# One tag for each buffer of a ring, and a last output chunk that is copied in halves and sent by two queues

## The chip, the core and the metric

The kernel runs on one core of one Trainium2 chip. The core has a matrix engine (TensorE, PE in the profile, with its weight loads as PEld), a vector engine (VectorE, DVE), a scalar engine (ScalarE, ACT), a general engine (GpSimd, POOL) and SyncE (SP), which here issues the DMAs. Each engine works through its own list of instructions in order and waits at semaphores for the others. The metric is the device time of one execution in microseconds; smaller is better.

## The reference

```python
def _attn_ref(q, k, v):                        # q, k, v: 8 batches x 8 heads x 1152 x 64
    q_pool = q.reshape(B, H, S // 2, 2, D).mean(axis=3)
    scores = (1.0 / np.sqrt(D)) * np.matmul(q_pool, k.transpose(0, 1, 3, 2))
    attn = np.exp(scores - scores.max(-1, keepdims=True))
    attn = attn / (attn.sum(-1, keepdims=True) + 1e-09)
    return np.matmul(attn, v)                  # 8 x 8 x 576 x 64

def _moe_ref(x, w_gate, wq, wk, wv, wo):       # x: 8 x 576 x 512, the heads side by side; 4 experts
    logits = x @ w_gate                        # the two best experts of a row, softmax over the two
    for e in range(E):
        q, k, v = x @ wq[e], x @ wk[e], x @ wv[e]          # 576 x 64 each
        a = softmax(causal(q @ k.T / np.sqrt(64)))
        out += weight[e] * (a @ v @ wo[e])     # weight is 0 where e is not among the two best
    return out                                 # 8 x 576 x 512, float32
```

## The kernel before, in words

The first stage is pooled attention. The 64 heads go in 32 pairs; a pair fills the 128 partitions with two heads of 64. For each pair the kernel finds row maxima (`f_max`, reduced by VectorE at line 572), computes transposed scores of nine key chunks (`f_st`, TensorE through `rows2`, line 325), takes exponentials on ScalarE into tiles named `pt` (line 666), multiplies them by v (`f_av`, TensorE through `cols2`, line 332) and adds up the `pt` tiles on GpSimd into `sacc` (line 349), from which the denominators come. `f_xfin` ends a half of a pair: ScalarE copies the accumulator out of PSUM into `accs`, TensorE sums `sacc` into a bank (called den here, line 332), VectorE transposes, inverts and multiplies it there (lines 722 to 734 and 345), ScalarE casts it into `x` and VectorE subtracts that cast from the same bank to get the low half of `x` (line 345). Only then is the bank of den free.

After every four pairs a batch of the second stage starts (`start_moe`): projections of x (`f_qk`, `f_vproj`, 12 matmuls at line 316 into one bank for each group), row maxima with the causal mask (`f_mmax`, line 956), scores, exponentials, products and at last the output projection (`f_out`). This work is laid between the attention work of the next four pairs.

All results of TensorE go to one ring of eight PSUM banks, `gen`, and all exponentials to one ring of eleven SBUF buffers, `pt`. A ring is an object of the kernel, and so is a planner: while the program is written out, `emit` keeps a clock for each engine and a time of last use for each buffer, and the main loop at the end of the kernel picks the next piece of work by these clocks and by the tables HEAD, CYCLE and TAIL. `Ring.new` takes the buffer that by the planner's clocks comes free first, `min(self.slots)`, and then asks the tile pool for a tile:

```python
r = Res(self.pool.tile(self.shape, self.dt, tag=self.tag, name=f"{self.tag}_{self.n}", bufs=self.bufs), self)
```

All buffers of a ring have one tag here, so which of the eight banks the tile really gets is the pool's choice and not the planner's. The first instruction that writes into the new tile waits until the last user of the old tile in that bank is done.

The output of the last batch is written by `f_out` in its tail form: a chunk of 128 rows is projected in two steps of three matmuls, ScalarE copies the 128x512 result into a `pt` buffer, and SyncE issues its DMA through `mv`. Chunks 2, 3 and 4 come last, in this order. Chunk 4 is made of 64 rows of the last batch and 64 of the one before, and so goes out in two DMAs of 64 rows.

Of the kernel before, what the change touches and what calls it, by code (L numbers as in the profile page):

```python
# [17 lines left out]
SQ = 576  # L18
# [6 lines left out]
DM = 512  # L25
# [9 lines left out]
AC0, ACL, ACT = 0.1, 0.8, 0.8  # L35
# [69 lines left out]
class Res:  # L105
# [15 lines left out]
        return self.u + SEM[self.ue]  # L121

    def free(self):
        self.ring.slots.append((self.ru, self.u, self.ue))
        self.ring.live -= 1


class Ring:
    def __init__(self, pool, tag, shape, dt, bufs):
        self.pool, self.tag, self.shape, self.dt, self.bufs = pool, tag, shape, dt, bufs  # L130
        self.slots, self.live, self.n = [(0.0, 0.0, "")] * bufs, 0, 0

    def avail(self, k=1):
        return sorted(self.slots)[k - 1][0] if len(self.slots) >= k else INF
# [1 line left out]
    def new(self):  # L136
        t = min(self.slots)
        self.slots.remove(t)
        self.live += 1
        self.n += 1  # L140
        r = Res(self.pool.tile(self.shape, self.dt, tag=self.tag, name=f"{self.tag}_{self.n}", bufs=self.bufs), self)
        _, r.u, r.ue = t
        return r


# [15 lines left out]
def pooled_attention_then_moe_kernel(ctx: ExitStack, tc: tile.TileContext, qT, kT, vP, wall, wop, out):  # L161
    nc = tc.nc
# [172 lines left out]
    def act_copy(o, i, n, R, W, psum=True):  # L335
        nc.scalar.copy(o, i)  # L336
        emit("ACT", n / 1200 + (0.05 if psum else 0.083), R, W)
# [23 lines left out]
    def fl(ap):  # L361
        return ap.bitcast(F32) if ap.dtype == F32R else ap

    def mv(dst, src, R, W):
        d = fl(dst)
        nc.sync.dma_start(d, fl(src))
        n = 4
        for k in d.shape:
            n *= k
        emit("SP", 0.63, R, W, n / 250e3)  # L370

    def sp():
        return clk["SP"] - (SP0 if prog["f"] == 0.0 else SPL if prog["f"] < NP - 0.9 else SPT)
# [678 lines left out]
    def f_yfin(b, ep, qb, acc, sacc):  # L1052
# [12 lines left out]
        if k < qn:  # L1065
# [5 lines left out]
            yl, o = YL[b // 2], 64 * (b % 2)  # L1071
# [3 lines left out]
        YR[b, ep, qb] = yr  # L1075
        if b == NB - 1:
            if (b, 1 - ep, qb) not in YR:
                for t in ((0, 1), (2, 3, 4))[qb]:
                    spawn("out", f_out(b, (t,), (ep, 1 - ep)), m_prio(b, 3))
        elif qb == 0 and (b, 1 - ep, 0) in YR:  # L1080
            spawn("out", f_out(b, range(4 + b % 2), (0, 1)), m_prio(b, 3, "C"))
# [4 lines left out]
    def f_out(b, ts, eps):  # L1086
        tail = b == NB - 1
        ro = r_pt if tail else r_ob
        for t in ts:
# [4 lines left out]
            ps, ob = r_gen.new(), ro.new()  # L1094
            o = ob.ap.rearrange("p a b -> p (a b)")[:, 0:DM] if tail else ob.ap
            for i, ep in enumerate(eps):
                if i and tail:
                    yield (lambda: yr(ep), "C")
                for k, (yi, W) in enumerate(((0, OH), (1, OH), (0, OL))):
                    l = YL[b // 2][:, ep, yi, :] if t == 4 else Y[b, ep][:, yi, 128 * t:128 * t + 128]  # L1100
                    mm(ps.ap, l, W[:, ep, :], i + k == 0, i == 1 and k == 2, 0.233, [YR[j, ep, q] for j in bs], [ps])
            m_prog[b] += 1.4
            act_copy(o, ps.ap, DM, [ps], [ob])
            ps.free()
            for i, j in enumerate(bs):
# [95 lines left out]
```

## Time and profile before

| | us |
|---|---|
| median of three runs | 1204.38 (1204.35 to 1204.39) |
| profiled execution, whole time | 1205.93 |
| profiled execution, span of the trace | 1204.2 |
| TensorE busy | 1158.4 (96%) |
| GpSimd busy | 972.0 (81%) |
| VectorE busy | 860.6 (71%) |
| ScalarE busy | 704.5 (58%) |
| mean granted TensorE clock | 0.996 of full speed |

The trace covers 1204.2 of the 1205.93 us of its execution; the median of the runs is 1.55 us below that execution. A row of the timeline gives start and duration in us, engine, line, operation, output<-inputs, shapes, how many instructions were merged, and in brackets the idle time of the engine ahead of it with the engine and line whose event ended it. A busy engine still need not be the one that sets the end, so the idle time of TensorE and the chain of work that ended last are read beside the shares.

### The profile page before, as it was taken

What the parts mean: (1) busy time and instruction counts of PE and PEld (TensorE: products, weight loads), DVE (VectorE), ACT (ScalarE), POOL (GpSimd) and SP (SyncE); (2) the same over time, 40 slices, a digit from 0 to 9 for tenths busy, and PEclk for the clock granted to TensorE, in tenths of its full rate; (3) what the DMA queues carried; (4) which work ended last, traced back from release to release, by engine and by line L of the source; (5) the groups of instructions that cost most, each with busy time, mean ns of one, the idle gap of its engine ahead of it and who ended that gap; (6) DMA issues with size and microseconds to landing.
All of it is one profiled execution on the core that took longest, in us unless ns stands there. A gap on an engine that the chain in (4) does not pass through costs nothing.

```text
span 1204.2 us, 29456 instructions
## 1 busy us (share of the span) xinstructions
PE 1158.4 (96%) x11233; PEld 892.0 (74%) x11233; DVE 860.6 (71%) x2113; ACT 704.5 (58%) x2036; POOL 972.0 (81%) x844
## 2 busy tenths in 40 slices
PE   6999999999999999999999999999999999999997
PEld 5676886778876787767886777866877677877785
DVE  7988667767676767777677776776767876577265
ACT  5676545765466654665556754566646665465624
POOL 4999978797699966999669987699786996889912
PEclk9999998999999999999999999999999999999999
DMA  4232212022211212122111221112211122200001
GB/s 158 80 102 69 61 54 67 16 66 76 61 54 55 69 48 61 54 60 92 32 41 54 85 82 30 44 47 85 78 41 34 60 65 87 61 15 9 8 29 45
DMA packets 40426, 70.30 MB, mean 58 GB/s; under 512 B 4871, under 2 KB 31453, under 8 KB 40285
## 3 DMA queue, kind: packets, MB, share of 16 engines
q1 hardware_dynamic: 40284, 68.43, 18.5%
q8 instruction: 88, 1.44, 0.5%
q14 instruction: 54, 0.43, 0.1%
HBM read 58.73 MB, written 9.44 MB: 57 GB/s over the span
## 4 chain that ended last, share of the span: by engine, by line
PE 61%; POOL 27%; DVE 5%; ACT 3%; issue 3%; DMA 1%; POOLq 0%; SPq 0%; DVEq 0%; ACTq 0%
PE gen L325 24%; POOL sacc L349 23%; PE gen L316 19%; PE gen L332 17%; POOL kl L349 3%; ACT pt L666 2%; POOL pt L1018 1%; DVE gen L956 1%; DVE PM L572 1%; DVE ql L345 1%; ACT pt L999 1%; PE gen L622 0%; DVE gen L734 0%; DMA qraw<-in_qT 0%; DVE gen L345 0%
## 5 line engine op out<-in xcount | busy, mean ns | idle before, releaser
L349 POOL TENSOR_TENSOR sacc<-sacc,pt 128x640 f32<-128x640 f32 (+4 forms) x588 | 828.2, 1413 | 128.6 <-ACT sacc L341 92.4
L572 DVE TENSOR_REDUCE PM<-gen 128x1 f32<-128x384 f32 x864 | 425.6, 549 | 168.7 <-PE gen L325 140.3
L666 ACT ACTIVATE pt<-gen 128x320 f32<-128x320 f32 (+1 forms) x1152 | 381.4, 432 | 137.1 <-PE gen L325 126.9
L332 PE MATMUL gen<-pt,v 128*64 128x320 f32 (+4 forms) x2752 | 355.7, 402 | 1.7 <-POOL pt L1018 0.5
L332 PEld LDWEIGHTS gen<-pt,v 128*64 128x64 f32 (+1 forms) x2752 | 192.1, 137 | 138.9 <-issue 11.8
L325 PE MATMUL gen<-qh,kh 64*128 64x320 f32 (+1 forms) x1152 | 211.8, 316 | 2.7 <-ACT accs L336 1.1
L325 PE MATMUL gen<-qh,kl 64*128 64x320 f32 (+1 forms) x1152 | 196.3, 297 | 0.0
L325 PE MATMUL gen<-RM,ON 64*128 64x320 f32 (+1 forms) x1152 | 191.6, 292 | 0.8 <-ACT RM L336 0.8
L325 PE MATMUL gen<-ql,kh 64*128 64x320 f32 (+1 forms) x1152 | 191.3, 293 | 0.0
L325 PE MATMUL gen<-kh,qh 64*128 64x384 f32 x768 | 157.1, 368 | 7.4 <-ACT qh L336 7.1
L325 PEld LDWEIGHTS gen<-qh,kh 64*128 64x128 f32 x1152 | 132.8, 185 | 33.8 <-issue 11.3
L325 PEld LDWEIGHTS gen<-RM,ON 64*128 64x128 f32 x1152 | 130.4, 186 | 1.2 <-ACT RM L336 1.0
L325 PEld LDWEIGHTS gen<-ql,kh 64*128 64x128 f32 x1152 | 129.8, 186 | 0.0
L325 PEld LDWEIGHTS gen<-qh,kl 64*128 64x128 f32 x1152 | 127.4, 186 | 0.0
L325 PEld LDWEIGHTS gen<-kh,qh 64*128 64x128 f32 x768 | 88.2, 187 | 38.1 <-issue 16.3
L316 PE MATMUL gen<-x,WH 128*128 128x320 f32 (+1 forms) x512 | 104.9, 299 | 7.4 <-DVE x L345 7.4
L349 POOL TENSOR_TENSOR kl<-kraw,kh 128x384 fp32r<-128x384 f32 x96 | 95.5, 1013 | 9.5 <-ACT mqh L336 3.4
L956 DVE CUSTOM_DVE_ANT_0 gen<-gen,mqk 64x288 f32<-64x288 f32 (+4 forms) x160 | 74.7, 503 | 25.6 <-PE gen L325 24.4
L316 PEld LDWEIGHTS gen<-x,WH 128*128 128x128 f32 x512 | 82.2, 188 | 10.6 <-issue 9.7
L332 PE MATMUL gen<-sacc,ones 128*64 128x320 f32 (+1 forms) x384 | 66.1, 425 | 13.8 <-POOL sacc L349 13.3
L336 ACT CAST x<-gen 128x256 fp32r<-128x256 f32 x64 | 25.8, 403 | 86.9 <-DVE gen L345 86.8
L316 PE MATMUL gen<-x,WL 128*128 128x320 f32 (+1 forms) x256 | 75.6, 295 | 0.0
(116 smaller groups left out, 1573.5 us busy)
## 6 DMA issues: line engine op xcount, KB each, us to landing
kraw<-in_kT SPq DMA_DIRECT2D x96, 192.0 KB
v<-in_vP SPq DMA_DIRECT2D x96, 192.0 KB
qraw<-in_qT SPq DMA_DIRECT2D x31, 576.0 KB
out<-ob SPq DMA_DIRECT2D x28, 256.0 KB
wst<-in_wall SPq DMA_DIRECT2D x8, 193.0 KB
out<-pt SPq DMA_DIRECT2D x4, 256.0 KB
RM<-nt SPq DMA_DIRECT2D x62, 2.5 KB
out<-ob SPq DMA_DIRECT2D x6, 128.0 KB
```

Source lines behind the costliest of these rows:

```text
L316: nc.tensor.matmul(o, lhsT, rhs, start=start, stop=stop)
L325: nc.tensor.matmul(o(j), l(HEAD[j]), r(HEAD[j]), start=i == 0, stop=i == len(terms) - 1)
L332: nc.tensor.matmul(o(HEAD[j]), l(j), r(j), start=start, stop=stop)
L336: nc.scalar.copy(o, i)
L345: nc.vector.tensor_tensor(o, a, b, op=op)
L349: nc.gpsimd.tensor_tensor(o, a, b, op=op)
L572: nc.vector.tensor_reduce(pm[:, i, t:t + 1], ps[:, :384], axis=AX.X, op=ALU.max)
L666: nc.scalar.activation(pts[i][:, j, :qn], st[j][:, qn * i:qn * i + qn], AF.Exp, scale=0.0625)
L956: nc.vector.tensor_tensor_reduce(p, p, mqk[:m, 384 + m - w:384 + m], 1.0, LOW, ALU.add, ALU.max, pm[:m, j, c, i:i + 1])
L999: nc.scalar.activation(pt_[:kn, j, f:qn], st[j][:kn, o - n:o], AF.Exp, scale=0.125)
L1018: nc.gpsimd.affine_select(out=sq, in_=sq, compare_op=ALU.is_ge, fill=0.0, base=0, pattern=[[0, 2], [1, kn]], channel_multiplier=-1)
```

## The change

Two things are changed.

The tag of a tile is now made of the ring's name and the number of the buffer that the ring chose, with one buffer for each tag. So the tile gets exactly the buffer that `min(self.slots)` names. To keep that number, a slot is a tuple of four, and `free` hands it back. The shapes and the number of buffers stay as they were. In the built programs 787 of the 2472 `gen` tiles and 97 of the 693 `pt` tiles follow another tile in their buffer than before; in all other rings each tile follows the same one. The work on each engine stands in the same order as before up to the last output chunks.

In the tail the chunks go in the order 2, 4, 3, so that a chunk of 128 full rows comes last. Its result is copied in halves of 256 columns, the first by ScalarE and the second by VectorE; SyncE sends the first half and ScalarE's own queue the second.

```diff
--- before.py
+++ after.py
@@ -121,14 +121,14 @@
         return self.u + SEM[self.ue]
 
     def free(self):
-        self.ring.slots.append((self.ru, self.u, self.ue))
+        self.ring.slots.append((self.ru, self.u, self.ue, self.slot))
         self.ring.live -= 1
 
 
 class Ring:
     def __init__(self, pool, tag, shape, dt, bufs):
         self.pool, self.tag, self.shape, self.dt, self.bufs = pool, tag, shape, dt, bufs
-        self.slots, self.live, self.n = [(0.0, 0.0, "")] * bufs, 0, 0
+        self.slots, self.live, self.n = [(0.0, 0.0, "", i) for i in range(bufs)], 0, 0
 
     def avail(self, k=1):
         return sorted(self.slots)[k - 1][0] if len(self.slots) >= k else INF
@@ -138,8 +138,9 @@
         self.slots.remove(t)
         self.live += 1
         self.n += 1
-        r = Res(self.pool.tile(self.shape, self.dt, tag=self.tag, name=f"{self.tag}_{self.n}", bufs=self.bufs), self)
-        _, r.u, r.ue = t
+
+        r = Res(self.pool.tile(self.shape, self.dt, tag=f"{self.tag}{t[3]}", name=f"{self.tag}_{self.n}", bufs=1), self)
+        _, r.u, r.ue, r.slot = t
         return r
 
 
@@ -361,13 +362,13 @@
     def fl(ap):
         return ap.bitcast(F32) if ap.dtype == F32R else ap
 
-    def mv(dst, src, R, W):
+    def mv(dst, src, R, W, by="SP"):
         d = fl(dst)
-        nc.sync.dma_start(d, fl(src))
+        (nc.sync if by == "SP" else nc.scalar).dma_start(d, fl(src))
         n = 4
         for k in d.shape:
             n *= k
-        emit("SP", 0.63, R, W, n / 250e3)
+        emit(by, 0.63, R, W, n / 250e3)
 
     def sp():
         return clk["SP"] - (SP0 if prog["f"] == 0.0 else SPL if prog["f"] < NP - 0.9 else SPT)
@@ -1075,7 +1076,7 @@
         YR[b, ep, qb] = yr
         if b == NB - 1:
             if (b, 1 - ep, qb) not in YR:
-                for t in ((0, 1), (2, 3, 4))[qb]:
+                for t in ((0, 1), (2, 4, 3))[qb]:
                     spawn("out", f_out(b, (t,), (ep, 1 - ep)), m_prio(b, 3))
         elif qb == 0 and (b, 1 - ep, 0) in YR:
             spawn("out", f_out(b, range(4 + b % 2), (0, 1)), m_prio(b, 3, "C"))
@@ -1100,6 +1101,17 @@
                     l = YL[b // 2][:, ep, yi, :] if t == 4 else Y[b, ep][:, yi, 128 * t:128 * t + 128]
                     mm(ps.ap, l, W[:, ep, :], i + k == 0, i == 1 and k == 2, 0.233, [YR[j, ep, q] for j in bs], [ps])
             m_prog[b] += 1.4
+            if tail and t == 3:
+
+                hs, w = [Res(None), Res(None)], DM // 2
+                act_copy(o[:, :w], ps[:, :w], w, [ps], [hs[0]])
+                nc.vector.tensor_copy(o[:, w:], ps[:, w:])
+                emit("DVE", w / 960 + 0.07, [ps], [hs[1]])
+                for i, by in enumerate(("SP", "ACT")):
+                    mv(out[b * SQ + 128 * t:b * SQ + 128 * t + 128, w * i:w * i + w], o[:, w * i:w * i + w], [hs[i]], [], by)
+                ps.free()
+                ob.free()
+                continue
             act_copy(o, ps.ap, DM, [ps], [ob])
             ps.free()
             for i, j in enumerate(bs):
```

Lines of the changed kernel are 1 to 12 higher than those of before from the second half of `Ring` on. In the rows below a name is a tile, the first number counts the tiles of its ring and the second is a running number; in brackets stand the semaphores that an instruction waits for.

The first place is on TensorE, about 313 us into the span, where a projection of batch 1 begins (`gen_659` and `gen_660` are its first two banks, after four maxima products of the batch before it). Before:

```order
L325 MATMUL gen_657_5019<-mkh_3_4475,mqh_3_4457 64x288 [waits DVE_49]
L325 MATMUL gen_658_5020<-mkh_3_4475,mqh_3_4457 64x288 [waits DVE_49]
L316 MATMUL gen_659_5029<-x_5_2154,WH_116 128x256 [waits DVE_49,PE_49]
L316 MATMUL gen_659_5029<-x_5_2154,WH_116 128x256
L316 MATMUL gen_659_5029<-x_5_2154,WL_117 128x256
L316 MATMUL gen_659_5029<-x_6_2863,WH_116 128x256 x2
L316 MATMUL gen_659_5029<-x_6_2863,WL_117 128x256
L316 MATMUL gen_659_5029<-x_7_3492,WH_116 128x256 x2
L316 MATMUL gen_659_5029<-x_7_3492,WL_117 128x256
L316 MATMUL gen_659_5029<-x_8_4095,WH_116 128x256 x2
L316 MATMUL gen_659_5029<-x_8_4095,WL_117 128x256
L316 MATMUL gen_660_5046<-x_5_2154,WH_116 128x320 [waits Activation_49]
```

and with the change:

```order
L326 MATMUL gen_657_5019<-mkh_3_4475,mqh_3_4457 64x288 [waits DVE_49]
L326 MATMUL gen_658_5020<-mkh_3_4475,mqh_3_4457 64x288 [waits DVE_49]
L317 MATMUL gen_659_5029<-x_5_2154,WH_116 128x256 [waits Activation_49]
L317 MATMUL gen_659_5029<-x_5_2154,WH_116 128x256
L317 MATMUL gen_659_5029<-x_5_2154,WL_117 128x256
L317 MATMUL gen_659_5029<-x_6_2863,WH_116 128x256 x2
L317 MATMUL gen_659_5029<-x_6_2863,WL_117 128x256
L317 MATMUL gen_659_5029<-x_7_3492,WH_116 128x256 x2
L317 MATMUL gen_659_5029<-x_7_3492,WL_117 128x256
L317 MATMUL gen_659_5029<-x_8_4095,WH_116 128x256 x2
L317 MATMUL gen_659_5029<-x_8_4095,WL_117 128x256
L317 MATMUL gen_660_5046<-x_5_2154,WH_116 128x320 [waits DVE_49]
```

The work is the same; the first matmul of `gen_659` waited for VectorE and TensorE and now waits for ScalarE, and that of `gen_660` waited for ScalarE and now waits for VectorE. In the built programs the bank of `gen_659` was that of `gen_652`, a den bank, and is now that of `gen_624`, an accumulator that ScalarE copies out; `gen_660` takes the den bank in its place. The same exchange stands at the first projection of batches 2 to 6 (`gen_968`, `gen_1276`, `gen_1585`, `gen_1893`, `gen_2202`).

The second place is on TensorE early in the kernel, at the scores of pair 4 about 109 us into the span (`gen_242` and `gen_243` take row maxima, `gen_244` and `gen_245` the scores of the two heads). Before:

```order
L325 MATMUL gen_242_1810<-kh_15_1480,qh_5_1374 128x384 [waits Activation_49]
L325 MATMUL gen_243_1811<-kh_15_1480,qh_5_1374 128x384 [waits Activation_49]
L325 MATMUL gen_244_1817<-qh_4_930,kh_10_710 128x320 [waits DVE_49]
L325 MATMUL gen_245_1818<-qh_4_930,kh_10_710 128x320 [waits DVE_49]
L325 MATMUL gen_244_1817<-qh_4_930,kl_10_1338 128x320
```

and with the change:

```order
L326 MATMUL gen_242_1810<-kh_15_1480,qh_5_1374 128x384 [waits Activation_49]
L326 MATMUL gen_243_1811<-kh_15_1480,qh_5_1374 128x384 [waits DVE_49]
L326 MATMUL gen_244_1817<-qh_4_930,kh_10_710 128x320 [waits Activation_49]
L326 MATMUL gen_245_1818<-qh_4_930,kh_10_710 128x320 [waits Activation_49]
L326 MATMUL gen_244_1817<-qh_4_930,kl_10_1338 128x320
```

The first matmuls of `gen_244` and `gen_245` waited for VectorE and now wait for ScalarE; with that of `gen_243` it is the other way round.

The third place is the end of the program. On SyncE, whose list holds the output DMAs (`pt_689` to `pt_693` are the five chunks of the last batch), the last five before:

```order
L366 DMA out_0<-pt_690_19203 128x512 [waits DMAHW0_49,Activation_49]
L366 DMA out_0<-pt_691_19225 128x512 [waits DMAHW1_49,Activation_49]
L366 DMA out_0<-pt_692_19230 128x512 [waits DMAHW2_49,Activation_49]
L366 DMA out_0<-pt_693_19235 64x512 [waits DMAHW3_49,Activation_49]
L366 DMA out_0<-pt_693_19235 64x512 [waits DMAHW4_49]
```

and with the change:

```order
L367 DMA out_0<-pt_690_19203 128x512 [waits DMAHW0_49,Activation_49]
L367 DMA out_0<-pt_691_19225 128x512 [waits DMAHW1_49,Activation_49]
L367 DMA out_0<-pt_692_19230 64x512 [waits DMAHW2_49,Activation_49]
L367 DMA out_0<-pt_692_19230 64x512 [waits DMAHW3_49]
L367 DMA out_0<-pt_693_19235 128x256 [waits DMAHW5_49,Activation_49]
```

The two DMAs of 64 rows now stand ahead of the last one, which carries half a chunk. ScalarE's list now ends with the DMA of the other half, behind its own copy of 128x256, and VectorE's list ends with a copy that it did not have:

```order
L735 STREAM_TRANSPOSE gen_2469_19207<-r9_96_19213 128x320 [waits DVE_49]
L346 TENSOR_TENSOR gen_2469_19207<-accs_96_19193,gen_2469_19207 128x320 [waits DVE_49]
L346 TENSOR_TENSOR y_16_19090<-gen_2469_19207,y_16_19090 128x256 [waits DVE_49,Activation_49]
L346 TENSOR_TENSOR yl_4_18031<-gen_2469_19207,yl_4_18031 128x64
L1108 COPY pt_693_19235<-gen_2472_19234 128x256 [waits Activation_49]
```

The last row is added; it waits for ScalarE.

## Rows read from the trace of the kernel before

**Rows 1.** The page: busy time, share of the span and instructions of each engine.

```profile
PE 1158.4 (96%) x11233; PEld 892.0 (74%) x11233; DVE 860.6 (71%) x2113; ACT 704.5 (58%) x2036; POOL 972.0 (81%) x844
```

**Rows 2.** The page: the chain that ended last, shares of the span by engine.

```profile
PE 61%; POOL 27%; DVE 5%; ACT 3%; issue 3%; DMA 1%; POOLq 0%; SPq 0%; DVEq 0%; ACTq 0%
```

**Rows 3.** Waits: engine, line and releaser; total us, times, longest us.

```profile
PE gen L332 <- POOL sacc L349: 13.3, 17, 1.6
PE gen L316 <- DVE x L345: 7.4, 6, 1.2
...
ACT pt L666 <- POOL sacc L349: 7.9, 9, 1.4
```

**Rows 4.** Timeline of all engines from 311.0 to 313.5 us.

```profile
311.10 1.82 DVE L345 TENSOR_TENSOR ql<-qraw,qh 128x576 fp32r<-128x576 f32 x1
...
311.40 0.76 PE L325 MATMUL gen<-mkh,mqh 64*128 64x512 f32 x6
311.55 0.43 ACT L336 COPY accs<-gen 128x320 f32<-128x320 f32 x1
312.84 0.41 DVE L345 TENSOR_TENSOR x<-gen,x 128x256 fp32r<-128x256 f32 x1
...
313.40 0.36 PE L316 MATMUL gen<-x,WH 128*128 128x256 f32 x1 [1.24 <-DVE x L345]
```

**Rows 5.** Timeline of TensorE at 314.8 us, where the second group begins.

```profile
314.89 0.31 PE L316 MATMUL gen<-x,WH 128*128 128x320 f32 x1
```

**Rows 6.** Timeline of GpSimd from 313 to 375 us, the rows with idle time.

```profile
324.60 0.23 POOL L871 TENSOR_TENSOR gate<-v,gate 128x20 f32<-128x20 f32 x1 [5.34 <-DVE gate L871]
...
330.40 1.27 POOL L349 TENSOR_TENSOR sacc<-sacc,pt 128x512 f32<-128x512 f32 x1 [1.24 <-ACT sacc L341]
```

**Rows 7.** Timeline of TensorE and its loads, single rows at five other places.

```profile
147.13 0.30 PEld L316 LDWEIGHTS gen<-x,WH 128*128 128x128 f32 x2 [0.28 <-DVE PM L572]
...
431.93 0.51 PE L316 MATMUL gen<-WH,x 128*128 128x260 f32 x2 [0.26 <-ACT pt L666]
...
723.26 0.30 PEld L316 LDWEIGHTS gen<-WH,x 128*128 128x128 f32 x2 [0.37 <-ACT pt L666]
...
1068.59 0.18 PEld L325 LDWEIGHTS gen<-mqh,mkh 64*128 64x128 f32 x1 [0.20 <-DVE PM L572]
...
1167.85 0.51 PE L316 MATMUL gen<-WH,x 128*128 128x260 f32 x2 [0.57 <-DVE MPM L956]
```

**Rows 8.** Timeline of TensorE from 108.6 to 112.2 us.

```profile
109.17 0.87 PE L325 MATMUL gen<-qh,kh 64*128 64x320 f32 x2
...
111.72 0.76 PE L332 MATMUL gen<-sacc,ones 128*64 128x320 f32 x4 [1.24 <-POOL sacc L349]
```

**Rows 9.** Timeline of ScalarE from 109 to 111 us.

```profile
110.08 0.77 ACT L666 ACTIVATE pt<-gen 128x320 f32<-128x320 f32 x2 [1.44 <-POOL sacc L349]
```

**Rows 10.** The chain in order of time, its last piece: start, us, what.

```profile
1199.63 0.58 ACT pt L336
```

**Rows 11.** Timeline from 1183 us on: copies of 128x256 out of PSUM.

```profile
1196.40 0.37 ACT L336 CAST y<-gen 128x256 fp32r<-128x256 f32 x1 [0.64 <-DVE gen L345]
...
1196.92 0.42 DVE L345 TENSOR_TENSOR y<-gen,y 128x256 fp32r<-128x256 f32 x1 [0.55 <-ACT yl L336]
```

**Rows 12.** Timeline of SyncE, the issues of the last three output DMAs.

```profile
1199.54 0.33 SPq L366 DMA_DIRECT2D out<-pt  x1
...
1200.24 0.55 SPq L366 DMA_DIRECT2D out<-pt  x1
...
1200.84 0.59 SPq L366 DMA_DIRECT2D out<-pt  x1
```

**Rows 13.** Line 366: issue durations in ns, least, median, most.

```profile
L366 SPq DMA_DIRECT2D out<-ob x34: 332/344/1426, 247.0 to 1149.7; - x34
```

**Rows 14.** Windows: busy time by engine, PEclk, DMA share, GB/s.

```profile
1200.50:1201.00 0.50, 0.00 (x0) 0.00 (x0) 0.00 (x0) 0.00 (x0) 0.00 (x0) 1.00 0.98 381
...
1202.50:1203.00 0.50, 0.00 (x0) 0.00 (x0) 0.00 (x0) 0.00 (x0) 0.00 (x0) 0.52 0.36 82
```

## The prediction

> **What bounds the kernel now.** I read the shares first: TensorE is busy 96% of the span, GpSimd 81%, VectorE 71%, ScalarE 58% [rows 1]. A busy share is an average, so the chain that ended last comes next: 61% of it is TensorE and 27% GpSimd [rows 2]. So there are stretches where TensorE sets the pace and others where it is GpSimd with its additions into `sacc`. A wait of TensorE that is taken away counts if nothing behind it runs into GpSimd. The third view is therefore who TensorE waits for [rows 3]. The longest group is 13.3 us in 17 waits for GpSimd's sums, which are data. The second is 7.4 us in 6 waits, 1.2 us each, in which the first matmul of a projection waits for VectorE's subtraction of the low half of x. That subtraction yields nothing that this projection reads: the low half belongs to a later pair. It is the last reader of a den bank, so this is a wait for a PSUM bank and not for data, and the choice of bank is what the change alters.
>
> **The change part by part.** *The six waits at the projections.* The timeline at the first of them shows the whole case [rows 4]. The last maxima matmul ends at 311.40 + 0.76 = 312.16. The projection starts at 313.40, after 1.24 us of idle time. VectorE is late because it first does an addition into `ql` of 1.82 us, and only then, from 312.84 to 313.25, the subtraction that frees the bank. The accumulator bank, which this tile gets now, is free when ScalarE's copy into `accs` is done, at 311.55 + 0.43 = 311.98, which is 0.18 us before TensorE gets there. So nothing of this wait is left: 6 x 1.24 = 7.4 us.
>
> What is late next? The den bank goes to the second group of the same projection. In the trace that group starts 314.89 - 313.40 = 1.49 us after the first [rows 4, 5]; without the wait it would start at 312.16 + 1.49 = 313.65. It can start 0.15 us after the bank is free (313.40 - 313.25 in the same rows), thus at 313.40. The cover is 0.25 us. If VectorE is later than that, the rest of its lateness comes back as a wait there. After that comes GpSimd: it is idle for 5.34 us up to 324.60 and again 1.24 us up to 330.40, waiting both times for work that hangs from these projections [rows 6], so it moves forward with TensorE. I take 7.4 whole.
>
> *The other `gen` tiles.* The built orders give 794 matmuls another wait than before, most of them in pairs that swap a bank freed by ScalarE for one freed by VectorE, a few tenths of a microsecond each, in both directions. Most of these gain or lose a little that the next wait for GpSimd's sums (17 of them [rows 3]) takes back, since its sums don't come earlier for it. I looked for places where the idle time before the matmul is ended by the user of the old bank, where the new one is long free, and where no such wait follows soon. There are five, with 0.28, 0.26, 0.37, 0.20 and 0.57 us of idle time, three of them on the loads and two on the matmuls [rows 7]. The sum is 1.68; a matmul behind an idle load loses somewhat less, so I take 1.4. The ends are 0 and 1.7.
>
> On the other side, at 109 us the new bank is worse. The scores of pair 4 start at 109.17 [rows 8]. Their new banks are freed by two exponentials, which ran from 110.08 to 110.85 because ScalarE had itself waited for GpSimd [rows 9]. That puts up to 1.7 us in TensorE's way. But 2.5 us later the same stretch ends in a wait of 1.24 us for GpSimd [rows 8], which doesn't get longer when TensorE comes later. And ScalarE's own wait there goes, see the next part. I take nothing for it; the ends are 0 and a loss of 1.7 - 1.24 = 0.5.
>
> *The `pt` tiles.* 97 of them change buffers. ScalarE waits 7.9 us in 9 waits for GpSimd to release a `pt` buffer [rows 3], and in the new program the waits of this kind name an addition that is older by up to four. ScalarE is busy 58% [rows 1], and TensorE has other work while an exponential is late, so I take nothing. The ends are 0 and a gain of 5.3, which is two thirds of those waits.
>
> *The tail.* Before: the last copy of 128x512 runs from 1199.63 to 1200.21 [rows 10]; SyncE issues chunk 3 at 1199.54, then the two halves of chunk 4 at 1200.24 (0.55 us) and 1200.84 (0.59 us) [rows 12]. Now chunk 4 stands where chunk 3 stood, so its two issues start at 1199.54 and end at 1199.54 + 0.55 + 0.05 + 0.59 = 1200.73. SyncE's half of chunk 3 follows at about 1200.77, against 1200.84 for the last issue before, so splitting the copy gains almost nothing on this queue: the queue is what is late. The issue itself covers 128 rows; such an issue takes 0.33 us, and one of 64 rows up to 0.59 [rows 12]: 0.26 less. For the other half, ScalarE's copy of 128x256 takes 0.37 us and ends at 1200.00. VectorE's copy waits for it, so the halves are not copied at the same time; with 0.42 [rows 11] it ends near 1200.45, and ScalarE issues at about 1200.5, done near 1200.8. That is ahead of SyncE's. So the gain is between 0.07 and 0.07 + 0.26; I take 0.2. No row shows an issue on ScalarE's queue. The longest issue of an output DMA on SyncE is 1.43 us [rows 13]; at that price ScalarE would end at 1200.5 + 1.43 = 1201.93, 0.5 us after 1200.84 + 0.59 = 1201.43. The ends of the tail are a loss of 0.5 and a gain of 0.3.
>
> The DMA engines of the core are 98% busy from 1200.5 to 1201.0 and 36% in the last half microsecond of traffic [rows 14], so it is not plain whether issue or transfer is late at the end. The Trainium skill (DMA: Bandwidth & Descriptors, section Issuing engines are not separate DMA queues) says that DMAs from several engines run on the same 16 DMA engines and that a second issuing engine saves only issue time. By that rule the tail would gain 0 where the transfers are late, and the whole sum would be smaller by the 0.2 that I take; no row here shows two queues at work.
>
> *The sum.* 7.4 + 1.4 + 0.2 = 9.0 us. The profiled span of 1204.2 (whole execution 1205.93) becomes 1195.2. The median of the runs lies 1.55 below that execution; the terms are differences and carry over, so 1204.38 - 9.0 = 1195.4.
>
> **The rivals.**
>
> *The wait moves to the second group.* For it: the cover is only 0.25 us, and VectorE's queue in front of the subtraction holds an addition whose length (1.82 us) leaves room to change. At each place where it happens, up to 1.24 - 0.25 = 1.0 us comes back. At all six: 9.0 - 6.0 = 3.0, thus 1201.4. Against it: VectorE's work there hangs from the den sum, which TensorE does earlier in the same stretch, so both move forward together.
>
> *GpSimd is the bound and takes the gain.* For it: 27% of the chain, 81% busy. Then the lead of TensorE is spent in longer waits for sums, and 8.8 of the 9.0 us go: about 1204.2. Against it: the idle time of GpSimd right behind each place, 5.34 and 1.24 us, is more than the 1.24 that would have to be absorbed.
>
> *Slower: the planner's clock names the wrong bank.* The new choice is only as good as the planner's clock, and at 109 us it is wrong by 1.7 us [rows 8, 9]. If such a place stood uncovered twice in each of the six cycles of four pairs, it would cost 12 x 1.7 = 20 and give 1204.4 + 20 - 9 = 1215.8; it decides from 6 places on (9.0 / 1.7 is 5.3). Against it: I find such losses over 0.3 us only in the first 222 us and one near the end, each covered by a longer wait that stands a few microseconds behind it.
>
> That the change doesn't take effect is ruled out by the order: the waits at the six places are others than before.
>
> **How the numbers follow.** The forecast has a chance of 0.79, the moved wait 0.11, GpSimd as the bound 0.06, the wrong banks 0.04. About 0.2%, which is 2.4 us, is what a measurement of this kernel can tell from no change. The first two cases lie below 1202.0, so faster has 0.90; same has 0.06 and slower 0.04. Low end: 7.4 + 1.7 + 0.3, and half of the bound for `pt`, 2.6, make 12.0, thus 1192.4. High end: the wait moved at three places (3.0), nothing from the other tiles (1.4), the early loss (0.5) and the tail at its worst (0.7) leave 9.0 - 5.6 = 3.4, thus 1201.0. That holds the forecast and a part of the first rival.
>
> **What would show it.** In the profile after, the group of TensorE's waits for VectorE's x subtraction is gone or down to a few tenths, and the projection follows the maxima matmuls without idle time. GpSimd's idle time before its `sacc` additions doesn't grow on TensorE's side: waits of TensorE for sums stay near 13 us. If they grow by 7, GpSimd is the bound. If the second group of a projection shows a wait for VectorE of about 1 us, the wait has moved. In the tail, ScalarE's issue stands beside SyncE's last one, and the end comes within 0.5 us of the last matmul's distance in the trace before (1204.2 - 1199.6). The forecast is wrong if TensorE's busy time itself changes, since no matmul is added or taken away.

## The result, and the profile after

The changed kernel takes 1192.78 us, the median of 5 runs (1191.47 to 1195.29), against 1204.38 us before: a ratio of 0.9904 with a 95% interval of 0.989 to 0.9919, or 11.6 us less. The forecast was 1195.4 with a range of 1192.4 to 1201.0. The time lies in the range, close to its low end: the sign and the largest term held, and 2.6 us more came than the sum had.

The profiled execution after took 1191.61 us with a span of 1189.9. The page's header, its shares and its chain by engine answer to [rows 1, 2]:

```profile
span 1189.9 us, 29438 instructions
PE 1151.2 (97%) x11233; PEld 890.1 (75%) x11233; DVE 857.1 (72%) x2114; ACT 703.7 (59%) x2036; POOL 974.9 (82%) x844
...
PE 60%; POOL 29%; ACT 4%; issue 3%; DVE 3%; DMA 0%; POOLq 0%; SPq 0%; ACTq 0%; DVEq 0%
```

VectorE's share of the chain fell from 5% to 3%, and GpSimd's rose from 27% to 29%: VectorE no longer stands between TensorE and the bank, and where TensorE came earlier GpSimd's additions are a little more often what ends last. The matmuls are as many as before. Of TensorE's waits in the changed kernel (us in total, times, the longest) these answer to [rows 3]:

```profile
PE gen L333 <- POOL sacc L350: 14.0, 17, 1.6
...
PE gen L326 <- ACT pt L667: 1.4, 1, 1.4
...
PE gen L317 <- ACT accs L337: 0.2, 1, 0.2
```

The group of 7.4 us for VectorE's x subtraction is gone. The waits for GpSimd's sums were 13.3 us in 17 and are now 14.0 in 17. The first of the six projections is this stretch of the timeline (start, duration, engine, line, operation, tiles), and it answers to [rows 4, 5]:

```profile
307.52 1.82 DVE L346 TENSOR_TENSOR ql<-qraw,qh 128x576 fp32r<-128x576 f32 x1
307.81 0.76 PE L326 MATMUL gen<-mkh,mqh 64*128 64x512 f32 x6
307.96 0.43 ACT L337 COPY accs<-gen 128x320 f32<-128x320 f32 x1
308.49 0.30 PEld L317 LDWEIGHTS gen<-x,WH 128*128 128x128 f32 x2 [0.22 <-ACT accs L337]
308.49 0.50 PE L317 MATMUL gen<-x,WH 128*128 128x256 f32 x2
...
309.25 0.41 DVE L346 TENSOR_TENSOR x<-gen,x 128x256 fp32r<-128x256 f32 x1
...
310.02 0.46 PE L317 MATMUL gen<-x,WH 128*128 128x320 f32 x2
```

VectorE does the same things in the same order: the addition into `ql`, then at 309.25 the subtraction, as late against the maxima matmuls as before. But the projection no longer stands behind it. It starts at 308.49, with the last of the maxima matmuls just ended (307.81 + 0.76 = 308.57, ends being modelled), on the bank that ScalarE's copy into `accs` left at 308.39. The den bank is free at 309.66, and its new user, the second group, comes at 310.02 without a wait. From the start of the maxima matmuls to the start of the projection it was 2.00 us [rows 4] and is 0.68: the step at this place is 1.32 us.

### The profile page after: what moved, and what is told of

It reads as the page before. It is cut to its first block, busy times and chain, and to the rows that moved or that the text cites. A ratio compares the mean times of both kernels' runs of the same rounds, so it can differ in the third digit from the quotient of the medians.

```text
span 1189.9 us, 29438 instructions
## 1 busy us (share of the span) xinstructions
PE 1151.2 (97%) x11233; PEld 890.1 (75%) x11233; DVE 857.1 (72%) x2114; ACT 703.7 (59%) x2036; POOL 974.9 (82%) x844
## 4 chain that ended last, share of the span: by engine, by line
PE 60%; POOL 29%; ACT 4%; issue 3%; DVE 3%; DMA 0%; POOLq 0%; SPq 0%; ACTq 0%; DVEq 0%
POOL sacc L350 25%; PE gen L326 23%; PE gen L317 19%; PE gen L333 18%; POOL kl L350 2%; ACT pt L667 2%; POOL pt L1019 1%; DVE PM L573 1%; ACT pt L1000 1%; PE gen L623 0%; ACT sacc L342 0%; DMA qraw<-in_qT 0%; POOL gate L872 0%; DVE gen L735 0%; DVE gen L346 0%
## 5 line engine op out<-in xcount | busy, mean ns | idle before, releaser
L326 PE MATMUL gen<-qh,kh 64*128 64x320 f32 (+1 forms) x1152 | 215.9, 315 | 2.7 <-ACT pt L667 1.4
L326 PE MATMUL gen<-qh,kl 64*128 64x320 f32 (+1 forms) x1152 | 200.6, 298 | 0.0
L326 PE MATMUL gen<-RM,ON 64*128 64x320 f32 (+1 forms) x1152 | 194.3, 292 | 0.8 <-ACT RM L337 0.8
L326 PE MATMUL gen<-ql,kh 64*128 64x320 f32 (+1 forms) x1152 | 194.1, 292 | 0.0
L326 PEld LDWEIGHTS gen<-qh,kh 64*128 64x128 f32 x1152 | 136.4, 185 | 32.1 <-issue 10.8
L326 PEld LDWEIGHTS gen<-RM,ON 64*128 64x128 f32 x1152 | 133.3, 186 | 1.2 <-ACT RM L337 1.1
L326 PEld LDWEIGHTS gen<-ql,kh 64*128 64x128 f32 x1152 | 132.7, 186 | 0.0
```

What stands on the lines that cost most here:

```text
L326: nc.tensor.matmul(o(j), l(HEAD[j]), r(HEAD[j]), start=i == 0, stop=i == len(terms) - 1)
```

## Experiments

A table first; the ratios are to the kernel before on the same chip. The granted clock of a run's span shifts its time by some tenths (see the end), so the last column has the median of the runs with a mean granted clock of 0.996 alone, where before has 1204.56 (8 runs). e8 has only one run of that kind.

| kernel | median us | ratio, 95% | at clock 0.996 |
|---|---|---|---|
| changed kernel | 1192.78 | 0.9904 (0.989 to 0.9919) | 1193.0 |
| e1 all tags, old tail | 1192.56 | 0.9906 (0.9891 to 0.992) | 1192.9 |
| e2 tail alone | 1204.66 | 1.0002 (0.9993 to 1.0011) | 1205.0 |
| e3 tags of `gen` alone | 1194.28 | 0.9921 (0.9908 to 0.9935) | 1194.3 |
| e4 tags of `pt` alone | 1203.88 | 1.0001 (0.9992 to 1.0009) | 1203.9 |
| e5 changed, six places undone | 1200.81 | 0.9967 (0.9955 to 0.998) | 1200.9 |
| e6 six places alone | 1196.80 | 0.9937 (0.9925 to 0.995) | 1196.8 |
| e9 six and five places | 1194.96 | 0.9922 (0.991 to 0.9934) | none |
| e10 six places and `pt` | 1196.67 | 0.9931 (0.9917 to 0.9944) | 1196.7 |
| e7 split chunk first | 1193.35 | 0.9904 (0.9889 to 0.9919) | 1193.4 |
| e8 halves, one queue | 1192.3 | 0.99 (0.9882 to 0.9918) | 1193.0 |

**Which part of the change does it.** The first three kernels take the parts alone. The tags without the tail:

```diff
-                for t in ((0, 1), (2, 4, 3))[qb]:
+                for t in ((0, 1), (2, 3, 4))[qb]:
...
-            if tail and t == 3:
-                ...
```

> The tags of the change, the tail of before. Theory (the whole gain is in the banks; the new tail itself costs about 0.4 us, since the end now comes 5.04 us after the last matmul against 4.67 before): about 0.4 us below the changed kernel, 1192.4, and 4.7 us from the last matmul to the end. Rival (the tail pays as I forecast): about 0.2 us above the changed kernel.

The tail without the tags:

```diff
-        r = Res(self.pool.tile(self.shape, self.dt, tag=f"{self.tag}{t[3]}", name=f"{self.tag}_{self.n}", bufs=1), self)
+        r = Res(self.pool.tile(self.shape, self.dt, tag=self.tag, name=f"{self.tag}_{self.n}", bufs=self.bufs), self)
```

> The tail of the change, one shared tag for each ring as before. Theory: the six waits of 1.24 us stay, the end comes 5.0 us after the last matmul, time 1204.8 against 1204.4. Rival (the tail pays): 1204.2.

And the tags on the PSUM ring `gen` alone, with the old tail:

```diff
+        own = self.tag in ('gen',)
+        tag, bufs = (f"{self.tag}{t[3]}", 1) if own else (self.tag, self.bufs)
+        r = Res(self.pool.tile(self.shape, self.dt, tag=tag, name=f"{self.tag}_{self.n}", bufs=bufs), self)
```

> Only the PSUM ring gets a tag for each buffer; all else as before. Theory (the banks are everything): within 0.5 us of the kernel with all tags, about 1192.5. Rival (the 2.4 us beyond my forecast come from the pt buffers, for which I took nothing): 1195.

Measured: e1 is as fast as the changed kernel (1192.56 against 1192.78), e2 as slow as the kernel before (ratio 1.0002), e3 has 10.3 of the 11.6 us at like clock. So the tail gives nothing, and the banks of `gen` most of it. Two expectations missed: e1's end stands 5.04 us behind the last matmul and not 4.7 (see the tail), and e3's 1194.3 is neither the 1192.5 of its theory nor the 1195 of its rival.

**The six places.** e5 is the changed kernel in which at each of the six projections the two tiles have their banks exchanged back, and nothing else; at these tile numbers the ring gives the tile the bank that the tile beside it would have had, and the two slots stay exchanged:

```diff
+BACK = {659: 652, 968: 961, 1276: 1269, 1585: 1578, 1893: 1886, 2202: 2195}
...
+        if self.tag == "gen" and self.n in BACK:
+            j = next(s for s in range(self.bufs) if self.tile[self.at[s]] == BACK[self.n])
...
+            self.at[i], self.at[j] = self.at[j], self.at[i]
...
```

> The changed kernel, in which the first group of the six projections gets the den bank again and the second group the accumulator bank (12 matmuls wait for another engine, nothing else differs). Theory (these six waits are 7.8 us and come back whole): six waits of 1.24 us for VectorE in the trace, 1200.6. Rival (the lead is lost further on in any case, or most of the gain comes from other tiles): at most three quarters of that, below 1198.6.

e6 is the other way round, the kernel before with nothing but these six exchanges: `gen` has a tag for each bank, and the bank of each tile is read from a list, which is that of the kernel before with two banks exchanged from these six tiles on.

```diff
+        own = self.tag == "gen"
+        tag, bufs = (f"gen{BANK[self.n - 1]}", 1) if own else (self.tag, self.bufs)
```

> The kernel before with the banks that its pool chose, and the exchange at the six projections alone (12 matmuls wait for another engine, nothing else differs). Theory: no wait of TensorE for the subtraction of x is left, 1204.4 - 7.8 = 1196.6. Rival (the wait moves to the second group, or GpSimd takes the lead back): 1201 to 1204.

In e5 the waits come back. The first two lines are its TensorE waits, the others the stretch of the timeline at the first of the six:

```profile
PE gen L341 <- POOL sacc L358: 13.9, 17, 1.6
PE gen L325 <- DVE x L354: 7.4, 6, 1.3
```

```profile
309.42 0.77 PE L334 MATMUL gen<-mkh,mqh 64*128 64x512 f32 x6
311.42 0.48 PE L325 MATMUL gen<-x,WH 128*128 128x256 f32 x2 [1.23 <-DVE x L354]
```

The projection starts 2.00 us after the maxima matmuls again, as in [rows 4]. In e6 the same stretch is that of the changed kernel, the group of waits for VectorE's x is gone, and the waits for sums stand first again:

```profile
309.00 0.77 PE L329 MATMUL gen<-mkh,mqh 64*128 64x512 f32 x6
309.70 0.50 PE L320 MATMUL gen<-x,WH 128*128 128x256 f32 x2
```

```profile
PE gen L336 <- POOL sacc L353: 14.1, 19, 1.7
```

At like clock e6 is 7.7 us faster than before (1204.56 to 1196.84) and e5 7.9 slower than the changed kernel (1193.0 to 1200.9). Matmul by matmul, the profiled execution of e5 falls behind that of e8 (further down, with the tags of the changed kernel and a clock of 0.996 as in e5) by 1.26 to 1.29 us at each of five of the six projections and by 1.06 at the one near 890 us: 7.4 in all. The 7.4 us of the six waits arrive at the end whole, from either side, and two rivals fall with that: the wait didn't move to the second group, and GpSimd didn't take the gain (the waits for sums stay at 14).

**The other `gen` tiles.** From e6 to e3 all other tiles of `gen` get their new banks: 1196.8 to 1194.3, another 2.5 us. e9 asks how much of it are the five places that the prediction picked out; it is e6, in whose list `BANK` two banks each are exchanged from the tiles 314, 917, 1534, 2255 and 2431 on as well.

> The kernel with the exchange at the six projections alone, and the same exchange at the five other places that the prediction named (147, 432, 723, 1069 and 1168 us; 10 more matmuls wait for another engine, nothing else differs). Theory (the five are worth their 1.4 us, and the rest of the 2.5 us that the other PSUM tiles gave lies at places that I had written off): 1195.4, that is 1.4 below the six alone at 1196.8. Rival (the five carry all of it): 1194.3. Second rival (they are taken back like the rest): 1196.8.

e9 has 1194.96, which is 1.8 less than e6, but its runs had a higher clock. The two profiled executions both ran at a granted clock of 0.999 with spans of 1194.5 and 1192.2. Matmul by matmul, e9's lead grows by 0.1, 0.3, 0.2, 0.2 and 0.5 us at the five places, some 1.2 in all; 0.3 us are there before the first of them, and the rest comes in small steps elsewhere. The forecast of 1.4 for these five was about right. The rest of the 2.5, 1.3 us by this count and 0.7 by the medians of e9 and e3, comes from tiles that I had written off. They don't stand at one place. The loads are where they show, as waits of a weight load that the old user of its bank ends. Some of the groups that changed most, first in e6, then in e3:

```profile
PEld gen L329 <- DVE PM L576: 11.9, 50, 0.5
...
PEld gen L329 <- ACT accs L340: 7.3, 15, 0.5
...
PEld gen L320 <- ACT pt L670: 5.5, 20, 0.5
...
PEld gen L329 <- ACT pt L670: 1.0, 3, 0.4
...
PEld gen L626 <- DVE PM L576: 0.4, 2, 0.2
```

```profile
PEld gen L328 <- DVE PM L575: 7.6, 32, 0.5
...
PEld gen L328 <- ACT accs L339: 2.5, 5, 0.5
...
PEld gen L319 <- ACT pt L669: 2.1, 10, 0.4
...
PEld gen L328 <- ACT pt L669: 4.7, 13, 1.7
...
PEld gen L625 <- DVE PM L575: 2.5, 8, 0.4
```

The first three groups lose 12.5 us, the last two gain 5.8. But other groups grow too, and all waits of loads that VectorE or ScalarE ended come to 61.1 us in e6 and 59.1 in e3: a net 2.0 us on the loads, beside 2.5 at the end. So the new banks are better at some tiles and worse at others, and only the balance shows.

**The `pt` tiles.** e4 has the tags on `pt` alone (the first of these edits, made to e3), e10 has them beside the six exchanges (the second, made to e6):

```diff
-        own = self.tag in ('gen',)
+        own = self.tag in ('pt',)
```

```diff
-        own = self.tag == "gen"
-        tag, bufs = (f"gen{BANK[self.n - 1]}", 1) if own else (self.tag, self.bufs)
+        own = self.tag in ("gen", "pt")
+        tag, bufs = (f"{self.tag}{BANK[self.n - 1] if self.tag == 'gen' else t[3]}", 1) if own else (self.tag, self.bufs)
```

> Only the ring pt gets a tag for each buffer; all else as before. Theory: ScalarE's waits for GpSimd to release a pt buffer shrink from 7.9 us to about 2.5, and the time stays at 1204.4, since TensorE has other work. Rival (the pt buffers carry the rest of the gain): 1202.

> The kernel with the exchange at the six projections alone, and a tag for each pt buffer; all other PSUM tiles as before. Theory (the pt buffers are worth something of their own, about 0.6 to 1.4 us, whatever the other banks): 1195.8. Rival (they pay only beside the other PSUM tiles): 1196.8.

Neither can be told from its partner without them: e4 from before (ratio 1.0001), e10 from e6 (1196.67 against 1196.80). But from e3 to e1, where all of `gen` has its tags, it is 1.7 us by the medians and 1.4 at like clock. The intervals of the two ratios overlap (0.9908 to 0.9935 and 0.9891 to 0.992), so the times alone don't separate the two. Of the 1.7 us between their two last matmuls in the profiled executions (both at 0.996) 0.5 are there by 40 us, and the rest builds up over the whole span. The size is uncertain. ScalarE's waits for GpSimd to release a `pt` buffer say why it can be so. They were 7.9 us in 9 waits before [rows 3]; in e4, in e3 and in e1 they are, in this order:

```profile
ACT pt L669 <- POOL sacc L352: 2.5, 4, 1.4
```

```profile
ACT pt L669 <- POOL sacc L352: 8.3, 8, 1.5
...
ACT pt L669 <- POOL pt L1021: 5.4, 4, 1.3
```

```profile
ACT pt L667 <- POOL sacc L350: 2.4, 4, 1.4
...
ACT pt L667 <- POOL pt L1019: 1.3, 1, 1.3
```

In e4 the tags take 5.4 us off these waits, and the end doesn't move: ScalarE's lateness is hidden there, as forecast. In e3, with TensorE earlier, ScalarE runs into `pt` buffers that GpSimd still reads, 13.7 us in all; the tags on `pt` take 10.0 of it. That some of it reaches the end is argued from these waits and not shown place by place; in e10 the tags take the same waits from the 9.7 us of e6 to 2.3, and the end doesn't move either. So `pt` is worth nothing by itself and, as far as these runs can tell, about 1.4 us behind the other change.

**The tail.** The end is measured from the end of the last matmul, since all ahead of it differs. The last matmul of before, then the changed kernel's tail, then the end of e1, which has the tags of the changed kernel and the old tail (timeline):

```profile
1199.15 0.39 PE L316 MATMUL gen<-OL,yl 128*128 128x512 f32 x1
```

```profile
1184.46 0.40 PE L317 MATMUL gen<-OL,y 128*128 128x512 f32 x1
1185.24 0.37 ACT L337 COPY pt<-gen 128x256 f32<-128x256 f32 x1 [0.40 <-PE gen L317]
1185.64 0.42 DVE L1108 COPY pt<-gen 128x256 f32<-128x256 f32 x1 [2.84 <-ACT pt L337]
1186.10 1.39 ACTq L367 DMA_DIRECT2D out<-pt  x1
```

```profile
1185.47 0.39 PE L317 MATMUL gen<-OL,yl 128*128 128x512 f32 x1
1186.25 0.59 ACT L337 COPY pt<-gen 128x512 f32<-128x512 f32 x1 [0.39 <-PE gen L317]
```

Before it is 1204.2 - (1199.15 + 0.39) = 4.66 us, after it 1189.9 - (1184.46 + 0.40) = 5.04: the end became 0.4 us longer. But in e1, with the old tail, it is 1190.9 - (1185.47 + 0.39) = 5.04 as well. So most of the 0.4 us comes with the tags on `pt` and not with the new tail. The old tail takes 4.66 to 4.72 us without these tags (before, e3, e6, e9) and 4.99 to 5.04 with them (e1, e4, e10); the new one takes 4.95 without them (e2) and 5.00 to 5.04 with them (e5 and the changed kernel).

With the tags on `pt` ScalarE's last copy starts 0.37 to 0.39 us after the last matmul, in all seven kernels that have them; in the five others it is 0.09 (in before the copy at 1199.63 [rows 10]). The chain of the changed kernel calls 0.33 of this "issue":

```profile
1184.91 0.33 issue
```

It isn't the buffer. In the built programs this copy waits in before and in the changed kernel for the same two things, the last matmul and a GpSimd addition, and GpSimd's last instruction had ended at 1177.68. What differs is the copy's place in ScalarE's list. With separate waits at semaphores counted as records, it is the 2624th record of ScalarE's trace in the seven kernels and the 2629th in the five. 2624 is 64 + 20 x 128, and the traces show a pause at such places: in all twelve together 70 instructions at the places 64, 192, 320 and so on stand directly behind a separate wait, and 65 of them start 0.32 to 0.36 us after it, the other five 0.20. At the places 128, 256 and so on there are 65 such instructions, of which 43 start after 0.04 us and none after more than 0.21. In the five kernels without the tags this place falls on a cast into `yl`, which starts while the cast ahead of it still runs, so nothing is lost there. What ScalarE does in the pause the profile doesn't show.

The issue of ScalarE's DMA took 1.39 us. In e2, where the copy is early, it took 0.38:

```profile
1197.95 0.40 PE L317 MATMUL gen<-OL,y 128*128 128x512 f32 x1
...
1199.31 0.38 ACTq L367 DMA_DIRECT2D out<-pt  x1
```

Yet e2 ends 1203.3 - 1198.35 = 4.95 us after its last matmul, so even with the copy and the issue early the new tail has no gain; it is 0.3 longer there than the old one of before. The next two kernels ask whether the issuing queue or the transfers are late. e8 sends both halves from SyncE's queue:

```diff
-                for i, by in enumerate(("SP", "ACT")):
+                for i, by in enumerate(("SP", "SP")):
```

> The changed kernel with both halves of the last chunk sent by SyncE. Theory (the second queue saves one issue, but halves land later than whole rows): the second half is issued 1.8 us after the last matmul and the end comes 5.5 us after it, 0.5 us later than with two queues. Rival (the two queues share the DMA engines and so win nothing): 5.0 us.

e7 is e1, with the old whole copies on SyncE's queue, and the chunk of two DMAs sent first (the edit against e1):

```diff
-                for t in ((0, 1), (2, 3, 4))[qb]:
+                for t in ((0, 1), (4, 2, 3))[qb]:
```

> All tags of the change; the tail of before, but with the chunk that goes out in two DMAs of 64 rows ahead of the two full chunks (4, 2, 3), each copied whole by ScalarE and sent by SyncE. Theory (SyncE's queue of issues and the landing behind its last one set the end): the last issue starts about 0.8 us after the last matmul instead of 1.3, and the end comes 4.0 us after it instead of 4.7 to 5.0, so about 0.8 us below the kernel with the tags alone. Rival (the transfers, not the issues, are late): the end stays 4.7 to 5.0 us after the last matmul.

Both expectations failed. e8, from which I had expected a longer tail (5.5 us), has this, with a span of 1191.3:

```profile
1185.73 3.05 SPq L367 DMA_DIRECT2D out<-pt  x5
...
1186.07 0.39 PE L317 MATMUL gen<-OL,y 128*128 128x512 f32 x1
1186.84 0.37 ACT L337 COPY pt<-gen 128x256 f32<-128x256 f32 x1 [0.39 <-PE gen L317]
```

It ends 1191.3 - 1186.46 = 4.84 us after the last matmul, with all issues on one queue, 0.2 sooner than with two queues. e7, whose last issue is over 1.82 us after the last matmul, against 2.18 in e1, ends after 4.96, against 5.04; I had expected 4.0. So from one arrangement to another the end hardly follows the issues: it is 4.7 to 5.0 us in all of them, and from the end of the last issue to the end of the span it is 2.4 us in the changed kernel, 2.5 in e8, 2.8 to 2.9 in before and e1, and 3.1 in e2 and e7. Within one arrangement it does follow: the late copy moves the issues and the end of the old tail by the same 0.3. In all twelve traces the last DMA packet is over 1.3 to 1.4 us ahead of the end of the span, so that much of the tail is neither issue nor transfer. What sets the landing in each arrangement stays open. Beside e8 stands the changed kernel: 4.84 us on one queue, 5.04 on two. The rule of the Trainium skill (DMA: Bandwidth & Descriptors, section Issuing engines are not separate DMA queues), that a second issuing engine saves issue time only, agrees with that.

## Why the prediction was right, and where its sum was not

*The six waits: 7.4, measured 7.7 to 7.9.* The reading of the timeline held at each step: the bank behind ScalarE's copy is free in time, the second group finds the den bank free, and the wait was for a bank and not for data. The cover of 0.25 us was enough. Counted as in the prediction, with 0.15 us from the free bank to the start, it was 310.02 - 309.66 - 0.15 = 0.21.

*The five other places: 1.4, measured about 1.2.* Right.

*All other `gen` tiles: 0, measured 0.7 to 1.3.* This step failed: "Most of these gain or lose a little that the next wait for GpSimd's sums (17 of them) takes back". Not all of it is taken back. From e6 to e3 the waits for sums went from 14.1 to 13.0 us, so they didn't take the gain. A likely reason, not shown, is that there are only 17 to 19 such waits in a span of 1200 us; between two of them gains of a tenth can add up.

*`pt`: 0, with an end of 5.3; measured 0 alone and about 1.4 with the rest.* The step "TensorE has other work while an exponential is late, so I take nothing" is true of the kernel before, as e4 shows, and not of the kernel with the new banks, as e3 shows: ScalarE's waits there are 13.7 us in place of 7.9. I had judged the cover of one part by the trace without the other part.

*The early place: 0.* Right. The changed kernel's rows there answer to [rows 8]:

```profile
109.89 0.74 PE L326 MATMUL gen<-qh,kh 64*128 64x320 f32 x2 [1.41 <-ACT pt L667]
...
111.05 0.76 PE L333 MATMUL gen<-sacc,ones 128*64 128x320 f32 x4
```

The new wait of 1.41 us is there, and the old wait for GpSimd behind it (1.24 us) is gone: one took the place of the other. The rival that such places are many, and not covered, doesn't hold: this is the only TensorE wait of that group, and the longest load wait of that kind is the same place. Smaller ones exist on the loads, up to 0.5 us each, as the last two groups of e3 above show; they are inside the 2.5 us.

*The tail: a gain of 0.2, measured a loss of 0.3 in the profile beside the early copy (e2), none beside e1, and nothing in the times.* The step that failed is "the queue is what is late". I worked the tail out from the issues, and from one arrangement to another the end doesn't follow them. One of the issues was mis-sized too: the last one on SyncE's queue, for 128 rows of half a chunk, was taken at 0.33 us and took 0.54 (1186.15 to 1186.69), so the 0.26 us of "less" weren't there. The sign was wrong; the ends (a loss of 0.5, a gain of 0.3) hold what was measured.

*The sum.* At like clock it is 7.7 for the six, 2.5 for all other `gen` tiles, the five places among them, and 1.4 for `pt`: 11.6, where 9.0 was forecast. The missing 2.6 us are 1.1 in the second and 1.4 in the third term, with 0.3 in the first, less the 0.2 of the tail. The time lies in the range because its low end had half of the bound for `pt`, 2.6 us, in it; the forecast itself had put that at nothing.

*A sign that was badly chosen.* "The forecast is wrong if TensorE's busy time itself changes": it changed, from 1158.4 to 1151.2 us with the same 11233 matmuls, and the forecast held. Part of it is the clock, below. Among profiled executions of like granted clock it still falls, 1157.8 in e2 to 1153.5 in e1, so the busy time of this view is no constant of a program. The rows of matmuls overlap: in before their durations add up to 3760 us within 1158 of busy time. A matmul that starts a tenth late, because its weight load waited, then shows no idle time, and the lost time counts as busy. That fits where the busy time fell: e5, which has all tags and the six waits, has 1154.2, and e10, which has none of the other `gen` banks, 1156.9. So this sign couldn't have told a wrong forecast from a right one.

## What to carry to other kernels

Where a ring of buffers has one tag, the pool picks the buffer and a planner's choice of slot is only a wish: for each wait on a buffer look up who frees it and whether that reader has anything to do with the work that waits. A gain that is read from idle time in front of TensorE holds if the next user of the late buffer comes after it is free and the next engine in the chain idles right behind; work that out at one place and count the places. Don't judge the cover of one part of a change by the trace before alone when another part makes the covering engine earlier, and at the end of a kernel measure from the last matmul to the end rather than adding up issues. Compare each part with the kernel that differs in that part alone: beside before the new tail looks 0.4 us longer, beside e1 it isn't.

## What the runs showed of the hardware

*TensorE's clock falls in some executions of a program and not in others.* In the profiled execution of before the granted clock is at its lower level (1.2 GHz) for a part of the stretch from 195 to 205 us; in that of the changed kernel it stays at 2.4 GHz. The windows view (stretch, length, busy time and count of each engine, granted clock, DMA share, GB/s), before and then after:

```profile
195.00:198.00 3.00, 2.27 (x10) 1.30 (x12) 2.97 (x13) 1.15 (x2) 1.56 (x2) 0.60 0.16 55
198.00:205.00 7.00, 7.00 (x38) 3.14 (x34) 3.93 (x13) 0.37 (x1) 6.69 (x5) 0.68 0.30 90
```

```profile
195.00:198.00 3.00, 2.66 (x19) 1.27 (x20) 3.00 (x12) 0.36 (x1) 2.49 (x2) 1.00 0.00 1
198.00:205.00 7.00, 7.00 (x80) 5.13 (x78) 4.19 (x15) 2.48 (x10) 6.69 (x5) 1.00 0.41 125
```

What TensorE does ahead of it is alike in both: short waits for VectorE's maxima, then the same matmuls. Before, then after:

```profile
195.74 0.38 PE L622 MATMUL gen<-ident,nm 128*10 128x128 f32 x1 [0.50 <-DVE MPM L956]
...
196.97 1.12 PE L332 MATMUL gen<-sacc,ones 128*64 128x256 f32 x4
197.88 7.26 PE L332 MATMUL gen<-pt,v 128*64 128x320 f32 x36
```

```profile
194.92 0.28 PE L623 MATMUL gen<-ident,nm 128*10 128x128 f32 x1 [0.50 <-DVE MPM L957]
...
195.95 0.65 PE L333 MATMUL gen<-sacc,ones 128*64 128x256 f32 x4
196.59 5.07 PE L333 MATMUL gen<-pt,v 128*64 128x320 f32 x36
```

The same 40 matmuls took 7.26 + 1.12 = 8.38 us there and 5.72 here: 2.66 us are this and not the change; by 218 us 2.3 of them are left, of the 14.3 between the two profiled spans, and 0.65 us more are there by 65 us. That is why the two profiles differ by more than the medians do. The profiled execution of e1 shows a lower clock at about 110 us too (0.87 from 105 to 118), that of the changed kernel doesn't, and up to the last output chunks the two programs are the same; so it is of the execution and not of the program. It also spreads the runs: the five of the changed kernel have 1191.47 and 1191.61 at a mean granted clock of 0.999, 1192.78 and 1193.15 at 0.996, and 1195.29 at 0.995. Differences of a microsecond in this kernel are to be read between runs of like clock.

*Behind a separate wait ScalarE starts late at every 128th place of its list.* An instruction directly behind a separate semaphore wait starts 0.04 us after it when nothing else holds it, and 0.32 to 0.36 us after it at the places 64, 192 and so on (65 of 70 cases in the twelve traces, the other five 0.20). In the seven kernels whose last copy stands at such a place, a packet of 8192 bytes of the instruction queue (q14 on the page) begins 0.64 to 0.83 us after the start of the copy. At the end of these seven kernels it is 0.3 us that no other work covers; in the five others, whose list has five more records ahead of the copy, nothing is lost at that place.

*A DMA issue has no fixed length.* ScalarE's one issue of the same half chunk took 0.38 us in e2 and 1.39 in the changed kernel. In both SyncE is issuing at about the same time (in the changed kernel three issues from 1184.87 to 1186.69); in e2 ScalarE's issue starts 0.29 us earlier against them. In the long case the packet of the instruction queue begins in the same stretch, 0.2 us ahead of the issue; in e2 none stands there. With two executions of the long kind (e5 has 1.36) and one of the short, this is an observation and no more.
